# A causal mask added by TensorE instead of selected by GpSimd, for the first two tiles of an mLSTM with two MLP stages

## The chip, the core and the metric

The program runs on one core of a Trainium2 chip. The core's engines have queues of their own and work them in order: TensorE (PE in the profile; its weight loads are PEld), VectorE (DVE), ScalarE (ACT), GpSimd (POOL) and SyncE (SP), which here only starts transfers. They wait for one another by semaphores. The metric is the time of one execution on the device, in microseconds (us).

## The reference

The kernel computes three stages one after the other. First an mLSTM layer with 2 batches, 8 heads, 768 steps and head size 40, then a mixture of 4 experts (320 to 1024 to 320, ReLU, weighted by normalized domain probabilities), then a gated MLP ((x w_a) * (x w_b)) w_out with inner size 1536. The mLSTM is a recurrence over the steps t; what matters here is its gating and its order:

```python
m_new  = max(f[t] + m, i[t])                 # running maximum
f_stab = exp(f[t] + m - m_new);  i_stab = exp(i[t] - m_new)
C = f_stab * C + i_stab * outer(v[t], k[t])
n = f_stab * n + i_stab * k[t]
y[t] = sigmoid(o[t]) * (C q[t]) / max(|n . q[t]|, 1)
```

Step t only sees steps up to t. In a form that works on 128 steps at once this is a causal mask.

## The kernel before

The 1536 rows (2 batches of 768) are 12 tiles of 128 steps; tiles 0 and 1 are the first 128 steps of the two batches. For each tile, and for each half of four heads (`hh`), the kernel makes a 128x512 block of scores k q (`scores`, tile `pt_c`) and a 128x512 block of exponents (`weights_of`, tile `pt_a`): TensorE multiplies `LT`, which holds the gate terms of the key steps, by `Rr`, which holds those of the query steps. ScalarE writes the exponential into `w_t`, GpSimd's `affine_select` sets the entries with a key later than the query to zero, VectorE multiplies by the scores (`s1b`), and TensorE multiplies by the values (`s2a`, tile `pt_y`). VectorE then divides (`s2b`), and three transposes (`s3a`) and a split into a high and a low part (`split_hi`, `split_lo`) give the operand `xh`, `xl` of the expert stage. That stage, and the gated MLP behind it, are long rows of products on TensorE (lines 207 to 263).

The gates come from a chain on VectorE: `gate1` is a scan for the running maximum `mr` along the steps, `gate2` a scan of the logarithmic decay, `gate_hi` and `gate3` split them for TensorE, and `build_R` fills `Rr`, in four calls for the first two tiles (two tiles by two halves). For the first tiles the scan starts from a column that GpSimd writes, line 402: `nc.gpsimd.memset(mr[:, 0:1], NEG)`, within `gate1`.

Order: the kernel runs under a manual schedule, so each engine's queue holds its instructions in the order in which the code writes them. The opening, from line 583 on, is written out by hand, and the rest is a list of events with due times among the expert stage's products. Ahead of the opening's scores stand ten warm-up products (`warm_up(WARM)`, line 590), products of zeros in bf16 whose result nobody reads; `wz`, their operand, lies in the last columns of the tile `sums` (named `acc` in the profile), which is used as a landing place for raw weights and later for the sums of the experts. Single warm-ups stand between later groups. The tile pools in PSUM are `ps_t` (four banks), `ps_a` and `ps_b` (two each).

Of the kernel before, what the change touches and what calls it, by code (L numbers as in the profile page):

```python
# [7 lines left out]
F32 = mybir.dt.float32  # L8
F32R = mybir.dt.float32r
BF16 = mybir.dt.bfloat16  # L10
# [4 lines left out]
ALU = mybir.AluOpType  # L15
# [3 lines left out]
P = 128  # L19
# [18 lines left out]
WARM = 10  # L38
# [3 lines left out]
NEG = -1.0e30  # L42
# [5 lines left out]
def mlstm_moe_kernel(ctx, tc, gates, qk, qc, kvo, dp, w1b, w2b, ident_d, bdmask_d, rsel_d, exp_d, out):  # L48
    nc = tc.nc
# [17 lines left out]
    sums = xp.tile([P, NT * DM], F32, name="acc")  # L67
# [199 lines left out]
    begun = {}  # L267
# [59 lines left out]
    ps_a = ctx.enter_context(tc.tile_pool(name="ps_a", bufs=2, space=PS))  # L327
    ps_b = ctx.enter_context(tc.tile_pool(name="ps_b", bufs=2, space=PS))
    with ExitStack() as c1:
# [4 lines left out]
        ps_t = c1.enter_context(tc.tile_pool(name="ps_t", bufs=4, space=PS))  # L334

        g_sb = {}
        td = {}
# [5 lines left out]
        LT = [ac.tile([G, P], F32R, name=f"LT{i}") for i in range(2)]  # L343
        Rr = [ac.tile([G, H, P], F32R, name=f"Rr{b}") for b in range(B)]
        dec = ac.tile([120, NCH, 3, B], F32, name="dec")

        def load_qk(n, hh, eng=None):

            t = td.setdefault(n, {})
            if 2 <= n < NP:  # L350
                t["qk", hh] = td[n - 2]["qk", hh]
            else:
                tag, bufs = ("qs", 2) if (n, hh) == (1, 1) else ("qk", QB)
                t["qk", hh] = qp.tile([KS, 2, 512], F32, tag=tag, name="qk_t", bufs=bufs)
            v = t["qk", hh].rearrange("p a b -> p (a b)")
            if n < 2:
                (nc.gpsimd if n else nc.vector).memset(v, 0.0)
            r = D if n < NP else KS
            (eng or nc.sync).dma_start(v[0:r], qk[n, hh, 0:r])
# [103 lines left out]
        def build_R(n, eng, h0=0, h1=H):  # L463
            j, b = n // 2, n % 2
            zx = g_sb[j]["zx"]
            eng.tensor_tensor(
                Rr[b][0:64, h0:h1], zx.bitcast(F32).unsqueeze(1).to_broadcast([64, h1 - h0, P]),
                rsel[0:64, b * H + h0:b * H + h1].unsqueeze(2).to_broadcast([64, h1 - h0, P]), op=ALU.mult)

        def weights_of(n, hh, pool=ps_t, tag="t"):  # L470

            j, b = n // 2, n % 2
            td[n]["w", hh] = w = qp.tile([P, 512], F32, tag="w", name="w_t", bufs=4)
            pa = pool.tile([P, 512], F32, tag=tag, name="pt_a")
            nc.tensor.matmul(pa, LT[j % 2], Rr[b][:, 4 * hh:4 * hh + 4, :].rearrange("p h t -> p (h t)"), start=True, stop=True)  # L475
            nc.scalar.activation(w, pa, AF.Exp)
            nc.gpsimd.affine_select(w, w, pattern=[[0, 4], [1, P]], compare_op=ALU.is_ge, fill=0.0, base=0, channel_multiplier=-1)

        def scores(n, hh, pool=ps_t, tag="t"):
            t = td[n]  # L480
            qs = t["qk" if n < NP else "qs", hh]
            t["pc", hh] = pc = pool.tile([P, 512], F32, tag=tag, name="pt_c")
            for h in range(4):
                hs = slice(h * P, (h + 1) * P)
                nc.tensor.matmul(pc[:, hs], qs[:, 1, hs], qs[:, 0, hs], start=True, stop=True, skip_group_check=True)  # L485

        def s1a(n, hh):
            weights_of(n, hh)
            scores(n, hh)
# [5 lines left out]
        def s2a(n, hh):  # L495

            j, b = n // 2, n % 2
            t = td[n]
            kv = t["kvo"]
            if hh == 0:  # L500
                t["py"] = ps_t.tile([P, 512], F32, tag="t", name="pt_y")
            for h in range(4 * hh, 4 * hh + 4):
                nc.tensor.matmul(  # L503
                    t["py"][:, h * DE:h * DE + 2 * DE], t["w", hh][:, (h % 4) * P:(h % 4 + 1) * P],
                    kv[:, NK + h * DE:NK + (h + 2) * DE], start=True, stop=True, skip_group_check=True)
            if hh == 1 and j > 0:
                pi = ps_t.tile([P, 512], F32, tag="t", name="pt_i")
                for g in range(3):
                    nc.tensor.matmul(pi[:, g * 123:(g + 1) * 123], t["qc"][:, g * P:(g + 1) * P], cbd[b][:, g, :], start=True, stop=True, skip_group_check=True)  # L509
                t["pi"] = pi  # L510

        def s2b(n):
            j, b = n // 2, n % 2
            t = td[n]
            r = og[j][:, b].rearrange("p (h d) -> p h d", d=D)
            y = a2.tile([P, H, DE], F32, tag="y", name="y_t", bufs=1)
            pyv = t["py"][:, 0:H * DE].rearrange("p (h e) -> p h e", e=DE)
            if j > 0:
                nc.vector.tensor_tensor(
                    y, t["pi"][:, 0:H * DE].rearrange("p (h e) -> p h e", e=DE),  # L520
                    g_sb[j]["ET"][:, b * H:(b + 1) * H].unsqueeze(2).to_broadcast([P, H, DE]), op=ALU.mult)
                nc.vector.tensor_tensor(y, pyv, y, op=ALU.add)
            else:
                y = pyv
            dn = a2.tile([P, H, 1], F32, tag="dn", name="dn_t")
            nc.vector.tensor_scalar(dn, y[:, :, D:DE], -1.0, 1.0, op0=ALU.mult, op1=ALU.max)
            nc.vector.tensor_tensor(dn, y[:, :, D:DE], dn, op=ALU.max)
            nc.vector.reciprocal(dn, dn)
            x = a2.tile([P, DM + 64], F32, tag="x", name="x_t")
            xv = x[:, :DM].rearrange("p (h d) -> p h d", d=D)  # L530
            nc.vector.tensor_tensor(xv, y[:, :, 0:D], dn.to_broadcast([P, H, D]), op=ALU.mult)
            t["last"] = nc.vector.tensor_tensor(xv, xv, r, op=ALU.mult).ins
            t["x"] = x
# [48 lines left out]

        ctx.enter_context(tc.manual_schedule())
        wz = sums[:, 3520:3776].bitcast(BF16)
        nc.gpsimd.memset(wz, 0.0)

        def warm_up(n):

            for _ in range(n):
                nc.tensor.matmul(pw, wz[:, 0:P], wz, start=True, stop=True)  # L590
# [25 lines left out]
        load_qk(0, 1)  # L616
        load_qk(1, 0)
        load_qk(1, 1)
        for t in LT:
            nc.vector.memset(t[0:64].bitcast(F32), 1.0)  # L620
        nc.sync.dma_start(td[0]["kvo"][:, NK:NK + NV], kvo[0, :, NK:NK + NV])
# [10 lines left out]
        nc.sync.dma_start(bdmask.rearrange("p g e -> p (g e)"), bdmask_d)  # L632
        nc.sync.dma_start(dpt.rearrange("p n e -> p (n e)"), dp)
        pw = ps_a.tile([P, 512], F32, tag="a", name="pt_w")
        warm_up(WARM)
        scores(0, 0)
        scores(0, 1)
        gate1(0, V)
        for b in range(B):
# [5 lines left out]
        for n in range(2):  # L645
            build_R(n, V, 0, 4)
            build_R(n, V, 4, 8)
        weights_of(0, 0, ps_b, "b")
        weights_of(0, 1, ps_b, "b")
        scores(1, 0)  # L650
        weights_of(1, 0, ps_a, "a")
        weights_of(1, 1, ps_b, "b")
        scores(1, 1)
        go(w1[:2])
        load_qk(2, 0)
# [11 lines left out]
        s2a(0, 0)  # L667
        s2a(0, 1)
        s2b(0)
        warm_up(1)  # L670
        s2a(1, 0)
        s2a(1, 1)
        warm_up(1)
# [74 lines left out]
        for k in range(NI * NCH):  # L748
            until(k)
            j, i = k // NI, k % NI  # L750
# [168 lines left out]
```

## Time and profile before

| | |
|---|---|
| median of 3 runs | 635.52 us (635.47 to 637.03) |
| the profiled execution's own time | 635.51 us |
| its span, first to last instruction | 633.8 us |
| PE busy, share of the span | 621.0 us, 98% |
| DVE | 419.4 us, 66% |
| ACT | 266.7 us, 42% |
| POOL | 186.0 us, 29% |
| chain that ended last, PE's share | 90% |

The busy shares are means over stages with different limits. From about 62 us on TensorE has work all the time; before that the mLSTM's first tiles pass through all engines in turn, and the engines wait for one another. The change is in the first 18 us. There the views that count are the timelines of the single engines: a row there gives start, length, engine, line, operation and what it reads and writes, and in brackets the idle time ahead of it and what ended that.

### The profile page before, as it was taken

Reading aid. Unit: us, or ns where it says so; the run is one execution under the profiler, and the core shown is the slowest. Engines: PE = TensorE matmul, PEld = TensorE weight load, DVE = VectorE, ACT = ScalarE, POOL = GpSimd, SP = SyncE. Lnnn points to the kernel's source line nnn. Section 1 sums busy time; section 2 is a strip of 40 time slices with the busy share of each in tenths; the row PEclk is TensorE's granted clock in tenths of the full one; section 3 lists DMA queues with packets and bytes.
Section 4 is the critical chain, followed back from the end, with each engine's and each line's share of the span. In section 5 each row is a group of like instructions: output and inputs, shape, how many; then the busy total and the mean of one; then the engine's idle time right before and its main releaser. Section 6 shows DMA issues by size and latency. Waiting matters only on the chain.

```text
span 633.8 us, 10305 instructions
## 1 busy us (share of the span) xinstructions
PE 621.0 (98%) x3799; PEld 553.1 (87%) x3799; DVE 419.4 (66%) x860; ACT 266.7 (42%) x592; POOL 186.0 (29%) x223
## 2 busy tenths in 40 slices
PE   9898999999999999999999999999999999999997
PEld 6788999999999888888888888888888888888886
DVE  8889959596753244332788887888656776854344
ACT  6665464646333233332433344544543433422121
POOL 4686342424111011233233333333222222220000
PEclk9998999999999999999999999999999999999999
DMA  7882443435203122323221222221111111000003
GB/s 218 240 231 74 116 118 95 120 99 125 55 12 78 35 69 58 79 59 109 57 71 54 71 57 68 70 64 44 45 54 35 55 36 35 19 1 1 1 3 123
DMA packets 27967, 46.77 MB, mean 74 GB/s; under 512 B 3285, under 2 KB 17869, under 8 KB 27917
## 3 DMA queue, kind: packets, MB, share of 16 engines
q1 hardware_dynamic: 27437, 45.33, 26.2%
q0 software_dynamic: 480, 0.79, 0.6%
q8 instruction: 30, 0.49, 0.3%
q14 instruction: 20, 0.16, 0.1%
HBM read 43.35 MB, written 1.97 MB: 72 GB/s over the span
## 4 chain that ended last, share of the span: by engine, by line
PE 90%; DVE 6%; ACT 2%; issue 1%; POOL 1%; ACTq 0%; DVEq 0%; POOLq 0%
PE psa L214 20%; PE psa L207 14%; PE psy L261 13%; PE psy L263 11%; PE psy L262 11%; PE psb L214 8%; PE pt_y L503 3%; PE pt_c L485 2%; PE psb L207 2%; PE psb L219 1%; PE psa L219 1%; PE pt_i L509 1%; PE pt_a L475 1%; PE pt_w L590 1%; PE pt_u L553 1%
## 5 line engine op out<-in xcount | busy, mean ns | idle before, releaser
L261 PE MATMUL psy<-wh,hh 128*128 128x320 f32 x528 | 169.1, 320 | 0.6 <-DVE acc L321 0.6
L263 PE MATMUL psy<-wh,hl 128*128 128x320 f32 x528 | 163.2, 309 | 0.0
L262 PE MATMUL psy<-wl,hh 128*128 128x320 f32 x528 | 163.1, 309 | 0.0
L261 PEld LDWEIGHTS psy<-wh,hh 128*128 128x128 f32 x528 | 99.6, 189 | 15.5 <-issue 12.1
L262 PEld LDWEIGHTS psy<-wl,hh 128*128 128x128 f32 x528 | 99.7, 189 | 2.6
L263 PEld LDWEIGHTS psy<-wh,hl 128*128 128x128 f32 x528 | 99.4, 188 | 0.0
L307 DVE SCALAR_TENSOR_TENSOR hl<-psa,hh 128x512 fp32r<-128x512 f32 x60 | 40.2, 689 | 74.4 <-ACT hh L306 73.9
L124 POOL TENSOR_TENSOR wl<-tp,lf 128x272 fp32r<-128x272 f32 x48 | 38.8, 808 | 122.2 <-DVE tp L123 122.2
L214 PE MATMUL psa<-xh,wh 128*128 128x512 f32 x246 | 70.1, 393 | 0.0
L207 PE MATMUL psa<-xh,wh 128*128 128x256 f32 (+1 forms) x258 | 65.8, 309 | 0.4 <-ACT xh L132 0.4
L306 ACT ACTIVATE hh<-psa 128x512 fp32r<-128x512 f32 x60 | 34.5, 597 | 72.4 <-PE psa L214 41.3
L207 PE MATMUL psa<-xh,wl 128*128 128x256 f32 (+1 forms) x258 | 63.9, 302 | 0.0
L237 ACT ACTIVATE hh<-psa 128x256 fp32r<-128x256 f32 x72 | 27.6, 383 | 75.0 <-PE psa L207 73.5
L312 DVE TENSOR_TENSOR g<-psa,bs 128x512 f32<-128x512 f32 x36 | 24.8, 688 | 49.3 <-ACT bs L310 35.0
L121 POOL TENSOR_TENSOR lf<-lf,sq 128x272 f32<-128x272 f32 x48 | 37.2, 776 | 67.8 <-ACT wh L120 34.0
L92 POOL TENSOR_TENSOR wl<-raw,wh 128x352 fp32r<-128x352 f32 x28 | 26.6, 956 | 96.4 <-ACT wh L90 83.9
L214 PE MATMUL psa<-xh,wl 128*128 128x512 f32 x164 | 51.2, 393 | 0.0
L214 PE MATMUL psa<-xl,wh 128*128 128x512 f32 x164 | 50.8, 391 | 0.0
L238 DVE SCALAR_TENSOR_TENSOR hl<-psa,hh 128x256 fp32r<-128x256 f32 x72 | 30.3, 420 | 30.7 <-ACT hh L237 30.4
L214 PEld LDWEIGHTS psa<-xh,wh 128*128 128x128 f32 x246 | 44.0, 188 | 6.0
L310 ACT COPY bs<-psb 128x512 f32<-128x512 f32 x36 | 21.1, 587 | 62.7 <-PE psa L220 35.0
L207 PEld LDWEIGHTS psa<-xh,wh 128*128 128x128 f32 x258 | 45.2, 191 | 2.1 <-ACT xh L132 0.7
(139 smaller groups left out, 1168.0 us busy)
## 6 DMA issues: line engine op xcount, KB each, us to landing
raw<-in_w2b SPq DMA_DIRECT2D x48, 272.0 KB, 2.8
qk_t<-in_qk SPq DMA_DIRECT2D x16, 480.0 KB, 6.9
raw<-in_w1b SPq DMA_DIRECT2D x40, 176.0 KB, 2.3
acc<-in_w1b SPq DMA_DIRECT2D x24, 176.0 KB, 3.5
kvo_t<-in_kvo SPq DMA_DIRECT2D x10, 364.5 KB, 4.8
og_t<-in_kvo SPq DMA_DIRECT2D x6, 320.0 KB, 5.7
out<-acc SPq DMA_DIRECT2D x12, 160.0 KB, 1.8
qc_t<-in_qc SPq DMA_DIRECT2D x10, 180.0 KB, 3.6
```

Source lines behind the costliest of these rows:

```text
L92: lo_eng.tensor_tensor(wl[:, cs], raw, wh[:, cs].bitcast(F32), op=ALU.subtract)
L121: nc.gpsimd.tensor_tensor(lf, lf, sq, op=ALU.mult)
L124: nc.gpsimd.tensor_tensor(wl[:, cs], tf, lf, op=ALU.add)
L207: nc.tensor.matmul(ps, l, r, start=(i == 0), stop=(i == len(prs) - 1))
L214: nc.tensor.matmul(ps, k(w, t), x[c][:, u, :], start=start and i == 0, stop=not start and i == len(prs) - 1)
L237: nc.scalar.activation(self.hh, ps, AF.Relu)
L238: nc.vector.scalar_tensor_tensor(self.hl, ps, 0.0, self.hh.bitcast(F32), op0=ALU.max, op1=ALU.subtract)
L261: nc.tensor.matmul(ps, lh, wh[:, off:off + DM], start=(fi == 0), stop=False)
L262: nc.tensor.matmul(ps, lh, wl[:, off:off + DM], start=False, stop=False)
L263: nc.tensor.matmul(ps, ll, wh[:, off:off + DM], start=False, stop=(fi == nf - 1))
L306: nc.scalar.activation(it.hh, ps, AF.Relu)
L307: nc.vector.scalar_tensor_tensor(it.hl, ps, 0.0, it.hh.bitcast(F32), op0=ALU.max, op1=ALU.subtract)
```

## The change

For tiles 0 and 1 the mask is no longer selected on `w_t` by GpSimd. Instead a block `mneg` (zero where the key is not later than the query, -1e30 elsewhere, bf16) is multiplied by an identity `idb` (bf16) into the bank `pt_a` first (`mask`), and the exponents product adds to it (`start=False`). GpSimd makes `mneg` and `idb` with two memsets and three selects, which the code writes behind the loads of q and k. Three masks take the place of three of the ten warm-ups, the fourth stands ahead of the last exponents product. The scores of tile 1's first half are issued in three parts (one head, one head, two heads) between the exponents products, and a warm-up between the value products of the two tiles is gone.

```diff
-            pa = pool.tile([P, 512], F32, tag=tag, name="pt_a")
-            nc.tensor.matmul(pa, LT[j % 2], Rr[b][...], start=True, stop=True)
+            begun = td[n].pop(("pa", hh), None)
+            pa = begun or pool.tile([P, 512], F32, tag=tag, name="pt_a")
+            nc.tensor.matmul(pa, LT[j % 2], Rr[b][...], start=not begun, stop=True)
             nc.scalar.activation(w, pa, AF.Exp)
+            if begun:
+                return
             nc.gpsimd.affine_select(w, w, pattern=[[0, 4], [1, P]], compare_op=ALU.is_ge, fill=0.0, base=0, channel_multiplier=-1)
+        def mask(n, hh, pool, tag):
+            td[n]["pa", hh] = pa = pool.tile([P, 512], F32, tag=tag, name="pt_a")
+            nc.tensor.matmul(pa, idb, mneg, start=True, stop=False)
...
+        mneg = sums[:, 3168:3424].bitcast(BF16)
+        idb = sums[:, 3776:3840].bitcast(BF16)
...
         load_qk(1, 1)
+        nc.gpsimd.memset(mneg, 0.0)
+        nc.gpsimd.affine_select(mneg, mneg, pattern=[[0, 4], [1, P]], compare_op=ALU.is_ge, fill=NEG, base=0, channel_multiplier=-1)
+        nc.gpsimd.memset(idb, 1.0)
+        nc.gpsimd.affine_select(idb, idb, pattern=[[1, P]], compare_op=ALU.is_ge, fill=0.0, base=0, channel_multiplier=-1)
+        nc.gpsimd.affine_select(idb, idb, pattern=[[-1, P]], compare_op=ALU.is_ge, fill=0.0, base=0, channel_multiplier=1)
...
-        warm_up(WARM)
+        warm_up(WARM - 3)
+        mask(0, 0, ps_b, "b")
+        mask(0, 1, ps_b, "b")
+        mask(1, 0, ps_a, "a")
         scores(0, 0)
         scores(0, 1)
         gate1(0, V)
...
-        weights_of(0, 0, ps_b, "b")
-        weights_of(0, 1, ps_b, "b")
-        scores(1, 0)
-        weights_of(1, 0, ps_a, "a")
-        weights_of(1, 1, ps_b, "b")
+        weights_of(0, 0)
+        scores(1, 0, h1=1)
+        weights_of(0, 1)
+        scores(1, 0, h0=1, h1=2)
+        weights_of(1, 0)
+        scores(1, 0, h0=2)
+        mask(1, 1, ps_b, "b")
+        weights_of(1, 1)
         scores(1, 1)
...
         s2b(0)
-        warm_up(1)
         s2a(1, 0)
```

GpSimd's queue before, from its first memset in the kernel on (`acc` at line 585 is the warm-ups' operand, `ISA` stands for pool configuration):

```order
L585 MEMSET acc 128x512
L607 MEMSET rmask 112x128
L608 MEMSET rmask 112x1
L357 MEMSET qk_t 120x1024 x2
L402 MEMSET mr 112x1
L477 ISA
L477 AFFINE_SELECT w_t<-w_t 128x512 x4
```

And the same place in the changed kernel, where lines 631 to 635 write `mneg` and `idb`, both named `acc`:

```order
L620 MEMSET rmask 112x1
L357 MEMSET qk_t 120x1024 x2
L631 MEMSET acc 128x512
L632 ISA
L632 AFFINE_SELECT acc<-acc 128x512
L633 MEMSET acc 128x128
L634 AFFINE_SELECT acc<-acc 128x128
L635 AFFINE_SELECT acc<-acc 128x128
L402 MEMSET mr 112x1
L92 TENSOR_TENSOR wl_147<-acc,wh_146 128x352 x5
```

The configuration and five new instructions stand ahead of the memset of `mr`, which stood ahead of them; the four selects on `w_t` are gone.

TensorE's queue before, from the last warm-up ahead of the scores to the value products of the two tiles (with buffer numbers; `Rr0` is of tile 0, `Rr1` of tile 1):

```order
L590 MATMUL pt_w_159<-acc_81 128x512
L485 MATMUL pt_c_170<-qk_t_123 128x128 x4
L485 MATMUL pt_c_175<-qk_t_126 128x128 x4
L475 MATMUL pt_a_209<-Rr0_108,LT0_106 128x512
L475 MATMUL pt_a_214<-Rr0_108,LT0_106 128x512
L485 MATMUL pt_c_218<-qk_t_129 128x128 x4
L475 MATMUL pt_a_224<-Rr1_109,LT0_106 128x512
L475 MATMUL pt_a_229<-Rr1_109,LT0_106 128x512
L485 MATMUL pt_c_233<-qk_t_132 128x128 x4
```

And in the changed kernel (line 485 there is the mask product, 476 the exponents, 495 the scores):

```order
L485 MATMUL pt_a_178<-acc_81 128x512
L495 MATMUL pt_c_180<-qk_t_123 128x128 x4
L495 MATMUL pt_c_185<-qk_t_126 128x128 x4
L476 MATMUL pt_a_174<-Rr0_108,LT0_106 128x512
L495 MATMUL pt_c_221<-qk_t_129 128x128
L476 MATMUL pt_a_176<-Rr0_108,LT0_106 128x512
L495 MATMUL pt_c_221<-qk_t_129 128x128
L476 MATMUL pt_a_178<-Rr1_109,LT0_106 128x512
L495 MATMUL pt_c_221<-qk_t_129 128x128 x2
L485 LDWEIGHTS acc_81
L485 MATMUL pt_a_232<-acc_81 128x512
L476 MATMUL pt_a_232<-Rr1_109,LT0_106 128x512
```

The exponents products are spread between the scores of tile 1's first half, and a mask product stands ahead of the last of them.

## Rows read from the trace of the kernel before

**Rows 1.** Chain of waits, first 20 us: start, length (us), what.

```profile
1.39 4.45 PE pt_w L590 x10
...
15.23 0.18 DVE dn_t L526
```

**Rows 2.** Timeline of VectorE, first 22 us: start, length, engine, line, operation.

```profile
3.47 0.48 DVE L406 TENSOR_TENSOR_SCAN mr<-gt,mr 112x128 f32<-112x128 f32 x1
...
7.39 2.49 DVE L466 TENSOR_TENSOR Rr<-zx,rsel 64x512 fp32r<-64x512 f32 x4
10.41 2.61 DVE L493 TENSOR_TENSOR w_t<-pt_c,w_t 128x512 f32<-128x512 f32 x4 [0.54 <-POOL w_t L477]
...
15.23 0.17 DVE L526 TENSOR_SCALAR dn_t<-pt_y 128x8 f32<-128x8 f32 x1 [0.23 <-PE pt_y L503]
```

**Rows 3.** Timeline of GpSimd, first 22 us.

```profile
0.81 0.53 POOL L585 MEMSET acc<- 128x512 bf16 x1 [0.29 <-POOLq L907]
1.26 0.21 POOL L607 MEMSET rmask<- 112x128 f32 x1
1.53 0.10 POOL L608 MEMSET rmask<- 112x1 f32 x1
...
3.34 0.10 POOL L402 MEMSET mr<- 112x1 f32 x1
9.39 2.89 POOL L477 TENSOR_SCALAR_AFFINE_SELECT w_t<-w_t 128x512 f32<-128x512 f32 x4 [5.96 <-ACT w_t L476]
```

**Rows 4.** Line 477, first 12 us: operation, ns min/median/max, first and last start.

```profile
L477 POOL TENSOR_SCALAR_AFFINE_SELECT w_t<-w_t x4: 634/638/983, 9.4 to 11.6; 128x512 f32<-128x512 f32 x4
L477 POOLq MODIFY_POOL_CONFIG  x2: 13/13/13, 3.4 to 3.4; - x2
```

**Rows 5.** Timeline of TensorE, first 22 us.

```profile
1.39 4.45 PE L590 MATMUL pt_w<-acc 128*128 128x512 bf16 x10 [1.39 <-POOL acc L585]
5.70 2.63 PE L485 MATMUL pt_c<-qk_t 120*128 120x128 f32 x16
8.21 1.02 PE L475 MATMUL pt_a<-Rr,LT 112*128 112x512 f32 x2
...
9.88 0.71 PE L475 MATMUL pt_a<-Rr,LT 112*128 112x512 f32 x2
10.43 1.05 PE L485 MATMUL pt_c<-qk_t 120*128 120x128 f32 x8
11.32 1.91 PE L503 MATMUL pt_y<-kvo_t,w_t 128*128 128x82 f32 x16
13.07 0.38 PE L590 MATMUL pt_w<-acc 128*128 128x512 bf16 x1
...
15.57 1.03 PE L590 MATMUL pt_w<-acc 128*128 128x512 bf16 x4
```

**Rows 6.** Timeline of ScalarE, first 45 us.

```profile
8.72 1.14 ACT L476 ACTIVATE w_t<-pt_a 128x512 f32<-128x512 f32 x2 [2.18 <-PE pt_a L475]
...
27.47 0.49 ACT L90 CAST wh<-acc 128x352 fp32r<-128x352 f32 x1 [1.66 <-DMA acc<-in_w1b]
```

**Rows 7.** Stretches: busy us (instructions) of each engine, granted clock, transfers.

```profile
core 0: us, PE busy (x) PEld busy (x) DVE busy (x) ACT busy (x) POOL busy (x), PEclk, DMA share, GB/s
6.00:7.00 1.00, 1.00 (x6) 1.00 (x6) 0.90 (x4) 0.52 (x2) 0.00 (x0) 1.00 0.95 221
7.00:8.00 1.00, 1.00 (x11) 1.00 (x11) 0.95 (x3) 0.00 (x0) 0.00 (x0) 1.00 1.04 233
...
58.00:62.00 4.00, 4.00 (x19) 4.00 (x20) 3.97 (x3) 1.62 (x4) 2.85 (x2) 0.57 0.00 0
62.00:66.00 4.00, 4.00 (x32) 3.89 (x31) 3.72 (x10) 1.78 (x6) 0.90 (x1) 1.00 0.86 207
```

**Rows 8.** Timeline of TensorE, first 60 us: its two long waits.

```profile
24.45 0.30 PE L454 MATMUL pt_e<-ident,ex 96*128 96x96 f32 x1 [1.99 <-ACT ex L444]
...
57.20 0.79 PE L457 MATMUL pt_e<-eb,expd 16*120 16x2 f32 x6 [2.54 <-POOL eb L448]
```

**Rows 9.** Timeline of SyncE, first 22 us.

```profile
15.14 0.90 SPq L86 DMA_DIRECT2D acc<-in_w1b  x2
```

More of the change, by code (lines that the diff above doesn't have):

```diff
@@ L473, in weights_of, with scores @@
             td[n]["w", hh] = w = qp.tile([P, 512], F32, tag="w", name="w_t", bufs=4)
-            pa = pool.tile([P, 512], F32, tag=tag, name="pt_a")
-            nc.tensor.matmul(pa, LT[j % 2], Rr[b][:, 4 * hh:4 * hh + 4, :].rearrange("p h t -> p (h t)"), start=True, stop=True)
+            begun = td[n].pop(("pa", hh), None)
+            pa = begun or pool.tile([P, 512], F32, tag=tag, name="pt_a")
+            nc.tensor.matmul(pa, LT[j % 2], Rr[b][:, 4 * hh:4 * hh + 4, :].rearrange("p h t -> p (h t)"), start=not begun, stop=True)
             nc.scalar.activation(w, pa, AF.Exp)
+            if begun:
+                return
             nc.gpsimd.affine_select(w, w, pattern=[[0, 4], [1, P]], compare_op=ALU.is_ge, fill=0.0, base=0, channel_multiplier=-1)
-        def scores(n, hh, pool=ps_t, tag="t"):
+        def mask(n, hh, pool, tag):
+            td[n]["pa", hh] = pa = pool.tile([P, 512], F32, tag=tag, name="pt_a")
+            nc.tensor.matmul(pa, idb, mneg, start=True, stop=False)
+        def scores(n, hh, pool=ps_t, tag="t", h0=0, h1=4):
             t = td[n]
             qs = t["qk" if n < NP else "qs", hh]
-            t["pc", hh] = pc = pool.tile([P, 512], F32, tag=tag, name="pt_c")
-            for h in range(4):
+            if h0 == 0:
+                t["pc", hh] = pool.tile([P, 512], F32, tag=tag, name="pt_c")
+            pc = t["pc", hh]
+            for h in range(h0, h1):
                 hs = slice(h * P, (h + 1) * P)
```

## The prediction

> **What bounds the kernel now.** I read the chain of waits first, over the first 20 us, since every instruction the change touches stands there. It is named almost wholly by TensorE: warm-up products from 1.39, the scores, the exponents, the value products, and from 15.23 VectorE's division [rows 1]. TensorE's own line hides a second chain that is as tight, so I read VectorE's timeline next. It has one gap of half a microsecond: the gate scan of the first two tiles starts at 3.47, the four builds of R end at 9.88 (7.39 + 2.49), the four products of scores and weights run from 10.41 to 13.02, and only the 0.54 us ahead of the latter are a wait, for GpSimd's mask [rows 2]. TensorE gets its first exponents product only at 8.21, after the first build of R (7.39 + 0.62 = 8.01); had it been quicker before, it would have waited there. So in this stretch the gate scan on VectorE sets the rest, and the question is what starts that scan.
>
> GpSimd's timeline answers it: it writes the first column of the running maximum (L402) at 3.34 to 3.44, right behind its two memsets of q and k, and the scan, which reads that column, starts 0.03 us after it [rows 2, 3]. The scan has no slack against GpSimd. Between that small memset and the first mask at 9.39 GpSimd shows 5.96 us of idle time. The line's own view shows what lies in it: two pool configuration instructions at 3.4, 13 ns each, which the program places ahead of the first select [rows 3, 4].
>
> **What the change removes.** Four selects of 0.64 to 0.98 us leave the way between exponential and product [rows 4]. VectorE's first product of scores and weights no longer waits until 10.41; it can follow the last build of R at 9.88. But TensorE does not wait for these products: it runs without a gap from the exponents product at 9.88 over the last scores (10.43) and the value products from 11.32 on, whose first operand would now be there at 10.6 and before was there at 11.1 [rows 2, 5]. So only what TensorE has to do itself counts. The exponents product of the last half tile still waits for the last R; ahead of it stand now, behind the R before (9.25, ready for TensorE at 9.45, as 8.21 followed 8.01), an exponents product (0.21), two heads of scores (0.44, half of the 0.89 from 10.43 to 11.32) and a mask (0.21): 10.31, where it could start at 10.08. The scores behind it start at 10.52, 0.09 later than before; the warm-up at 13.07 between the value products is gone (0.21; the same figure for a mask comes from the group of four warm-ups, (1.03 - 0.38) / 3). The gain at the second division is thus 0.1 to 0.2 us; I take 0.2. The three masks ahead of the scores replace three warm-ups of the same shape and cost nothing, as long as their operands are there.
>
> **What it adds, and where.** Five GpSimd instructions now stand ahead of the small memset L402. A memset of 128x512 bf16 took 0.53; a select of 512 elements 0.64 when nothing disturbed it; a memset of 128 elements 0.21; two selects of 128 elements lie between 0.10 (the shortest GpSimd row) and 0.64, and I take 0.25, near the quarter of the long one [rows 3, 4]. Each waits for the one before: 1.53 against 1.26 + 0.21 gives 0.06, three times. Sum 0.53 + 0.64 + 0.21 + 0.50 + 0.18 = 2.06, bounds 1.8 to 3.2. Queued behind them on GpSimd is the memset that the gate scan waits for, and behind the scan the whole of VectorE's queue. So the gate chain is late by 2.1 us from this alone.
>
> With the first select the pair of configuration instructions also moves ahead of that memset. What they set going has no row of its own. The bounds: nothing (their rows are 13 ns), or all the time up to the first select, whose start was at 9.39 and which took 0.35 longer than its fellows; 9.39 + 0.35 - 3.4 = 6.3 us [rows 3, 4]. I take 6.0, by the 5.96 us idle row: it is the only one in which this pair is followed by a select, under the same DMA load. Before, this time lay beside VectorE's gate work (3.47 to 8.01) and ScalarE's first exponential (from 8.72 on), so it cost nothing; that cover is gone now, because the memset for the scan stands behind it [rows 2, 6].
>
> The Trainium skill, "GPSIMD Engine Reference", section "Instruction dispatch", says that the first call to a freshly loaded kernel pays some 6 us (5.95 measured) for loading code, without an instruction in the profile. By that figure the sum below would be 643.15; this case's trace cannot confirm it, it only leaves room for it.
>
> The scan is late by 2.1 + 6.0 = 8.1; of the first memset's 0.53 some may lie beside the loading, so I take 8.0. It starts at 11.5, the first R is there at 16.0.
>
> TensorE meanwhile: seven warm-ups at 0.43 end at 4.4, then it has nothing until the identity is ready, at about 11.3. It will be at 1.2 GHz again or still: in the trace before, the warm-ups came 0.43 apart from 1.39 on, and the score products went from six starts in the microsecond 6 to 7 to eleven in the next, after 5.6 us of unbroken work (the granted clock column reads 1.00 from the start, so I go by the spacing of the rows) [rows 5, 7]. At that rate three masks (1.3) and 16 score instructions at 0.21 (3.4) take it from 11.3 to 16.0. The first R comes at 16.0 too, so the slow rate is just hidden; I add 0.2 for the products right behind it.
>
> **The sum.** 8.0 - 0.2 + 0.2 = +8.0 at the second division. Little downstream absorbs it: VectorE, ScalarE and GpSimd work their queues in order, and what shifts with them ends TensorE's two long waits (2.0 for ScalarE's exponential at 24.45, 2.5 for GpSimd at 57.20) [rows 8]. Only work that waits for a transfer gains; there is one such wait, 1.66 us on ScalarE ahead of 27.47, and it is not on the chain [rows 6]. I take 0.3 back for it. SyncE's queue holds one transfer (the second piece of block 1) until the last mask product has read its operand, near 18.7 instead of its issue before 16.04 [rows 9]; what is behind it (q and k of the next tiles) is late by about 3 us, less than its readers. From about 62 us on TensorE is the bound [rows 7], and it keeps the shift to the end. The profiled execution took 635.51 with a span of 633.8 (the median of the runs is 635.52): 635.51 + 8.0 - 0.3 = 643.2.
>
> **Rivals.**
> *The loading is short or is no loading at all.* Then only the 2.1 us of GpSimd work is late: 2.1 - 0.2 - 0.3 = +1.6, 637.1, which is within 0.3% (1.9 us; about what a measurement of this kernel can tell from no change). For it: the configuration rows are 13 ns, and the idle row is put down to ScalarE's exponential, which begins at 8.72 and, with a pair in 1.14, ends only shortly before the select. Against it: nothing in the trace runs on GpSimd in these 6 us, so it shows no short load either. It decides below about 0.3 us of loading. Chance 0.13. In between, a load of 0.3 to 4.5 us gives 637.4 to 641.6: 0.10.
>
> *TensorE's clock becomes the bound.* After 7 us without work, and with gaps while it waits for each R, it may stay at 1.2 GHz through the last scores and the value products: 0.89 + 3.5 us of work at twice the time is up to +4.4; half of that gives 645.4. For it: 16 scores took 2.63 where later eight took 1.05 [rows 5]. Against it: from 11.3 to 16 it has unbroken work as it had before 7.0. Chance 0.11.
>
> *Faster.* The set-up is hidden after all, the 0.2 is kept, and the low clock at 58 to 62 (0.57 granted, 19 instructions where the next 4 us have 32) does not come back, because the wait ahead of it falls otherwise: at the half rate that is (1 - 0.57) x 4 = 1.7 us at most [rows 7]. Time 635.5 - 0.2 - 1.7 = 633.6, just over 0.3%. It needs the scan not to wait for GpSimd; 0.03 us of slack speak against that. Chance 0.04.
>
> **Numbers.** Forecast: 643.2, chance 0.62, its own range 641.2 to 645.2 (loading 4.5 to 6.3, the low clock at 58 us gone or doubled). The range for 8 in 10 reaches down into the middle case, to 638.0, and up into the clock case, to 645.5; left out are the short load and the faster case (0.17) and a little above. Faster 0.04; within 0.3% 0.11; slower 0.85.
>
> **What would show it.** In the changed profile: a row of GpSimd's first select at or after 9.3, not at 4; the small memset behind it at about 11; VectorE's scan at about 11.5 with an idle time of 8 us ended by GpSimd; TensorE idle from 4.4 to about 11; the four products of scores and weights directly behind the builds of R, waiting for nothing on GpSimd; the second division at 22 to 23. If the first select starts near 4 and the scan at 5.6, the loading term is wrong. If the scan is at 3.5, the order of GpSimd's queue doesn't matter and the prediction fails at its root. If the scan is late as said and the end is not, something downstream had slack that I did not see.

## The result and the profile after

The changed kernel takes 639.22 us (median of 12 executions, 637.63 to 644.33), the kernel before 637.0 us (12 executions, 635.45 to 638.91) in the same comparison: ratio 1.0052, interval 1.0028 to 1.0076. It is slower by about 2.2 us at the median, not by 7.7; the mean rises by 3.3 us (636.70 to 639.95), since more executions lie on high steps. The times of both lie on steps: before 635.5, 637.05 and 638.8; after 637.65, 639.2, 641.0, 642.4 and 644.3. The lowest step rose by 2.2 us (637.63 against 635.45). The profiled execution of after took 639.18 with a span of 637.4, so it lies on the second step.

GpSimd's timeline, which answers to [rows 3]; start, length, engine, line, operation:

```profile
3.34 0.53 POOL L631 MEMSET acc<- 128x512 bf16 x1
3.94 0.64 POOL L632 TENSOR_SCALAR_AFFINE_SELECT acc<-acc 128x512 bf16<-128x512 bf16 x1
4.52 0.21 POOL L633 MEMSET acc<- 128x128 bf16 x1
4.79 0.29 POOL L634 TENSOR_SCALAR_AFFINE_SELECT acc<-acc 128x128 bf16<-128x128 bf16 x1
5.16 0.29 POOL L635 TENSOR_SCALAR_AFFINE_SELECT acc<-acc 128x128 bf16<-128x128 bf16 x1
5.40 0.10 POOL L402 MEMSET mr<- 112x1 f32 x1
```

The memset that the gate scan waits for is at 5.40, not at 3.34 [rows 3]. The first select starts at 3.94 and not at 9.4 or later. The view of its line shows the pair of configuration instructions right ahead of it (operation, ns min/median/max, first and last start):

```profile
L632 POOLq MODIFY_POOL_CONFIG  x2: 16/16/16, 3.8 to 3.8; - x2
...
L632 POOL TENSOR_SCALAR_AFFINE_SELECT acc<-acc x1: 637/637/637, 3.9 to 3.9; 128x512 bf16<-128x512 bf16 x1
```

VectorE's timeline, against [rows 2]:

```profile
5.53 0.48 DVE L406 TENSOR_TENSOR_SCAN mr<-gt,mr 112x128 f32<-112x128 f32 x1 [2.18 <-POOL mr L402]
...
9.45 2.49 DVE L466 TENSOR_TENSOR Rr<-zx,rsel 64x512 fp32r<-64x512 f32 x4
11.86 2.68 DVE L503 TENSOR_TENSOR w_t<-pt_c,w_t 128x512 f32<-128x512 f32 x4
...
15.53 0.17 DVE L536 TENSOR_SCALAR dn_t<-pt_y 128x8 f32<-128x8 f32 x1 [0.99 <-PE pt_y L513]
...
17.31 0.17 DVE L536 TENSOR_SCALAR dn_t<-pt_y 128x8 f32<-128x8 f32 x1
```

The scan is late by 2.06 (5.53 against 3.47), the first build of R by 2.06 (9.45 against 7.39), the second division by 2.08 (17.31 against 15.23). The wait for GpSimd's mask ahead of the products (0.54 before) is gone, as the change means it to be, and nothing comes of it at the second division.

TensorE's timeline, against [rows 5, 8]:

```profile
1.39 3.17 PE L602 MATMUL pt_w<-acc 128*128 128x512 bf16 x7 [1.39 <-POOL acc L597]
5.51 1.46 PE L485 MATMUL pt_a<-acc 128*128 128x512 bf16 x3 [0.95 <-POOL mr L402]
6.76 3.62 PE L495 MATMUL pt_c<-qk_t 120*128 120x128 f32 x16
10.28 0.71 PE L476 MATMUL pt_a<-Rr,LT 112*128 112x512 f32 x1
...
12.69 1.05 PE L495 MATMUL pt_c<-qk_t 120*128 120x128 f32 x8
...
26.64 0.30 PE L454 MATMUL pt_e<-ident,ex 96*128 96x96 f32 x1 [2.00 <-ACT ex L444]
...
27.58 1.86 PE L495 MATMUL pt_c<-qk_t 120*128 120x128 f32 x8
...
60.95 0.79 PE L457 MATMUL pt_e<-eb,expd 16*120 16x2 f32 x6 [2.55 <-POOL eb L448]
```

The masks wait 0.95 us for the identity. (The profile names L402, GpSimd's last instruction before they start; what they read is written by L635, which ends at 5.45.) Sixteen scores take 3.62 instead of 2.63, but the first exponents product follows its R as closely as before: 10.28 after a build that starts at 9.45, against 8.21 after 7.39. So the slow scores are hidden. Eight scores take 1.86 at 27.58, where eight took 1.05 before [rows 5]. Stretches (as [rows 7]) show why:

```profile
core 0: us, PE busy (x) PEld busy (x) DVE busy (x) ACT busy (x) POOL busy (x), PEclk, DMA share, GB/s
...
28.00:32.00 4.00, 4.00 (x24) 4.00 (x24) 2.41 (x4) 1.66 (x5) 4.00 (x5) 0.59 0.47 132
58.00:62.00 4.00, 1.45 (x12) 1.22 (x11) 3.96 (x5) 1.70 (x5) 3.92 (x5) 1.00 0.10 36
62.00:66.00 4.00, 4.00 (x21) 3.97 (x20) 3.94 (x4) 1.45 (x4) 2.61 (x2) 0.58 0.00 0
```

The granted clock is 0.59 from 28 to 32 us, behind the 2.00 us wait that ends at 26.64. VectorE's instructions are 2.2 us behind those of before up to 27 us and 3.7 us behind from 45 us to the end: that fall costs 1.5 us, the height of one step of the times. The low stretch at 62 to 66 is the one that stood at 58 to 62 before [rows 7].

### The profile page after: what moved, and what is told of

It reads as the page before. It is cut to its first block, busy times and chain, and to the rows that moved or that the text cites. A ratio compares the mean times of both kernels' runs of the same rounds, so it can differ in the third digit from the quotient of the medians.

```text
span 637.4 us, 10300 instructions
## 1 busy us (share of the span) xinstructions
PE 623.8 (98%) x3798; PEld 555.9 (87%) x3799; DVE 419.0 (66%) x860; ACT 266.9 (42%) x592; POOL 185.3 (29%) x224
## 4 chain that ended last, share of the span: by engine, by line
PE 90%; DVE 5%; ACT 2%; POOL 1%; DMA 1%; issue 1%; ACTq 0%; POOLq 0%; DVEq 0%
PE psa L214 20%; PE psa L207 14%; PE psy L261 12%; PE psy L263 11%; PE psy L262 11%; PE psb L214 8%; PE pt_y L513 3%; PE pt_c L495 2%; PE psb L207 2%; PE psb L219 2%; PE psa L219 1%; DMA gt<-in_gates 1%; PE pt_i L519 1%; PE pt_a L476 1%; PE pt_u L563 1%
```

## The experiments

Ratios are to the kernel before, executed beside each; e12 is a single execution. Two theories stood for the 2.2 us. By the queue theory the scan is late since five instructions stand ahead of its memset. By the TensorE theory the masks wait for their operands, and the scores then run at half rate.

**e1, the memset first.** On the changed kernel, line 402's memset goes ahead of the five:

```diff
...
         load_qk(1, 1)
+        mr0 = a2.tile([G, P + 1], F32, tag="mr", name="mr")
+        nc.gpsimd.memset(mr0[:, 0:1], NEG)
         nc.gpsimd.memset(mneg, 0.0)
```

> The changed kernel with only GpSimd's small memset for the scan (first column of mr) moved ahead of the five set-up instructions; the masks on TensorE still wait for the set-up. Queue theory (the late scan is the whole loss): scan back at 3.47, second division at 15.2 to 15.4, time at the level of the kernel before (635.5 where TensorE's clock falls once, 637.0 where it falls twice). TensorE theory (its scores, late behind the masks and at the half rate until 10.8, hold it as much as the scan does): first exponents product still at 10.2 to 10.3, second division at 16.7 to 17.0, time 637.0 to 637.4 with one fall of the clock.

Lowest time 636.04, median 639.18, ratio 1.0025 (1.0004 to 1.0046). The second division is at 15.72, 0.3 behind the range of the queue theory and 1.0 ahead of that of the TensorE theory. VectorE's timeline and GpSimd's beside it show what is left:

```profile
3.47 0.48 DVE L404 TENSOR_TENSOR_SCAN mr<-gt,mr 112x128 f32<-112x128 f32 x1
3.99 0.76 DVE L407 TENSOR_TENSOR lf<-gt,mr 112x128 f32<-112x128 f32 x1
4.78 0.29 DVE L408 TENSOR_TENSOR lf<-lf,mr 112x128 f32<-112x128 f32 x1
...
7.86 1.28 DVE L464 TENSOR_TENSOR Rr<-zx,rsel 64x512 fp32r<-64x512 f32 x2
```

```profile
3.97 0.63 POOL L632 TENSOR_SCALAR_AFFINE_SELECT acc<-acc 128x512 bf16<-128x512 bf16 x1
...
4.83 0.40 POOL L634 TENSOR_SCALAR_AFFINE_SELECT acc<-acc 128x128 bf16<-128x128 bf16 x1
```

The scan is back at 3.47. The instruction behind it takes 0.76 us instead of 0.29, beside GpSimd's select, and R comes 0.47 late for that reason. At the lowest step 1.6 of the 2.2 us are thus the memset's place (637.63 to 636.04); the median stays, since ten of the twelve executions lie on higher steps.

**e2, the set-up earlier.** The memset of `mr` and the five go ahead of the memsets of q and k, and the loads of tile 1 go later.

```diff
...
         nc.gpsimd.memset(rmask[:, 0:1], 0.0)
+        mr0 = a2.tile([G, P + 1], F32, tag="mr", name="mr")
+        nc.gpsimd.memset(mr0[:, 0:1], NEG)
+        nc.gpsimd.memset(mneg, 0.0)
...
-        load_qk(1, 0)
-        load_qk(1, 1)
...
         nc.sync.dma_start(td[1]["kvo"][:, NK:NK + NV], kvo[1, :, NK:NK + NV])
+        load_qk(1, 0)
+        load_qk(1, 1)
```

> The changed kernel with mr's memset and the whole set-up moved ahead of GpSimd's two memsets of tile 1's q and k, whose loads go behind those of the first values. Both theories: masks right behind the warm-ups at 4.4, scan at 3.4 to 3.5, first exponents product at about 8.2, second division at 15.0 to 15.2, 635.3 to 635.5 with one fall of the clock, so 2.1 to 2.3 under the changed kernel. If it stays above 15.6, the exponents, scores and masks in their new order cost TensorE something of their own, or the later loads of tile 1 do (then a wait ahead of its first scores shows it).

Lowest 635.95, median 637.62, ratio 1.0004 (0.9986 to 1.0023). The second division is at 15.91, above the 15.6 of the expectation, for two reasons. The collision only moves: VectorE's line 415 takes 0.59 instead of 0.23, beside GpSimd's memsets of q and k, which now start at 3.65.

```profile
4.97 0.59 DVE L415 TENSOR_SCALAR lf<-lf 112x128 f32<-112x128 f32 x1
```

```profile
3.65 1.84 POOL L357 MEMSET qk_t<- 120x1024 f32 x2
```

R comes 0.36 late by it (7.75). And the later loads of tile 1 cost what the expectation named as their sign, a wait ahead of its first scores:

```profile
9.39 0.46 PE L493 MATMUL pt_c<-qk_t 120*128 120x128 f32 x2 [0.33 <-DMA qk_t<-in_qk]
```

**e3, the delay alone.** The kernel before with four memsets of 128x512 ahead of line 402, and nothing else of the change:

```diff
...
         load_qk(1, 1)
+        for _ in range(4):
+            nc.gpsimd.memset(sums[:, 3168:3424].bitcast(BF16), 0.0)
```

> The kernel before, with four memsets of 128x512 bf16 on GpSimd (some 2.2 us) ahead of mr's memset and nothing else. Queue theory: scan at 5.7, second division 2.2 later than before (17.4), 637.7 with one fall of the clock: the loss of the change without any of its masks. TensorE theory: TensorE is free at 8.3 here, so only the scan counts, also 17.4. If the selects that the change removes were worth 0.2 behind a late scan, this kernel is 0.2 to 0.4 slower than the changed one, whose scan is 0.15 earlier. If VectorE's lateness were absorbed somewhere downstream, the time would stay under 637.

Median 642.97 (638.18 to 644.93), ratio 1.0066 (1.0041 to 1.0091). The delay alone costs more than the change, and more than the 637.7 that was expected. The scan is at 5.68; then TensorE waits 2.56 us for the first R, and its clock falls:

```profile
10.42 1.01 PE L475 MATMUL pt_a<-Rr,LT 112*128 112x512 f32 x2 [2.56 <-DVE Rr L466]
11.26 1.82 PE L485 MATMUL pt_c<-qk_t 120*128 120x128 f32 x8
```

```profile
11.00:15.00 4.00, 4.00 (x18) 3.77 (x19) 2.48 (x5) 2.48 (x5) 2.35 (x4) 0.57 1.02 332
```

The lowest time is 2.7 us above the kernel before, 0.5 more than the delay of R (9.59 against 7.39); the median is 4.8 higher still, since the clock falls (e9 below separates the two). In the profile of after no such wait stands ahead of R: the slow scores fill it.

**e4, ten warm-ups.** e1 with ten warm-ups instead of seven, to fill the wait ahead of the masks:

```diff
-        warm_up(WARM - 3)
+        warm_up(WARM)
```

> As the first of these (mr's memset ahead of the set-up), with ten warm-ups instead of seven ahead of the masks, so that TensorE works without a gap from 1.4. Queue theory: like that one, 15.2 to 15.4. TensorE theory, by the rate: the rate rises near 7.0 as in the kernel before, scores end at 8.8 to 9.0, second division at 15.5 to 15.8, about 1.2 us earlier than with seven warm-ups, 635.8 to 636.1 with one fall of the clock. TensorE theory, by the late masks alone: no earlier than with seven warm-ups (16.7 to 17.0), since three more products stand in the queue.

Lowest 636.01, median 637.61, ratio 1.0009 (0.9992 to 1.0026). The second division is at 15.71, within what the TensorE theory by the rate had named, but that theory asked for 1.2 us less than with seven warm-ups, and e1 has 15.72. The gap ahead of the masks costs nothing up to there, so the TensorE theory falls in this form. The median is 1.6 us under e1's; the two intervals overlap, so whether the gap brings on falls of the clock later stays open.

**e5, no selects.** What is the removal of the selects worth at most? This kernel leaves out the causal mask of tiles 0 and 1 altogether.

```diff
             nc.scalar.activation(w, pa, AF.Exp)
+            if n < 2:
+                return
             nc.gpsimd.affine_select(w, w, pattern=[[0, 4], [1, P]], compare_op=ALU.is_ge, fill=0.0, base=0, channel_multiplier=-1)
```

> The kernel before with the causal mask of tiles 0 and 1 left out altogether (no select, no mask product): what the removal alone is worth. Theory of the recorded prediction (TensorE's own work from the last R to the second division sets the time, the selects lie beside it): VectorE's four products start at 9.9 instead of 10.4, second division at 15.0 to 15.25, 635.3 to 635.5 with one fall of the clock. Rival (the select was on the way): second division at 14.2 to 14.7, 634.5 to 635.0.

Lowest 635.49, median 638.08, ratio 1.0009 (0.9992 to 1.0025). VectorE's products follow R without a wait, 0.62 us earlier than before, and the second division stays where it was (15.22 against 15.23):

```profile
9.79 2.50 DVE L495 TENSOR_TENSOR w_t<-pt_c,w_t 128x512 f32<-128x512 f32 x4
...
15.22 0.17 DVE L528 TENSOR_SCALAR dn_t<-pt_y 128x8 f32<-128x8 f32 x1 [0.24 <-PE pt_y L505]
```

TensorE sets that division, and the selects were hidden beside it. Their removal had nothing to win there.

**e6, the change without its cost.** The mask in 128 columns, read four times; its set-up ahead of the memsets of q and k; one of these on ScalarE; the first head of tile 1's scores ahead of the first exponents.

```diff
...
+            if (n, hh) == (1, 1):
+                nc.scalar.copy(v.rearrange("p (a b) -> p a b", b=256), sums[0:KS, 3520:3776].unsqueeze(1).to_broadcast([KS, 4, 256]))
...
+            nc.tensor.matmul(pa.rearrange("p (h t) -> p h t", h=4), idb, mneg.unsqueeze(1).to_broadcast([P, 4, P]), start=True, stop=False)
...
-        weights_of(0, 0)
         scores(1, 0, h1=1)
+        weights_of(0, 0)
```

> The changed kernel with the scan's memset first, the mask set-up in 128 columns instead of 512 (the product reads it four times), done ahead of GpSimd's memset of tile 1's first q and k, the second of these memsets on ScalarE, and the first head of tile 1's scores ahead of the first exponents product. So GpSimd has nothing left beside VectorE's gate chain. If the late scan (2.1) and GpSimd's slowing of VectorE's two-operand instructions (0.47 in the kernel with mr's memset first) were the whole loss: scan at 3.4 to 3.6, first build of R at 7.4 to 7.5, second division at 14.9 to 15.2, 635.2 to 635.5 with one fall of the clock, no or hardly any gain over the kernel before. If the removal is worth more than that, under 635.0. If something else in the change costs time, above 635.9.

Lowest 635.55, median 636.42, ratio 0.9997 (0.9976 to 1.0018). Scan at 3.45, R at 7.36, second division at 15.23: the loss is gone, and no gain stands in its place.

```profile
3.45 0.49 DVE L406 TENSOR_TENSOR_SCAN mr<-gt,mr 112x128 f32<-112x128 f32 x1
...
15.23 0.17 DVE L536 TENSOR_SCALAR dn_t<-pt_y 128x8 f32<-128x8 f32 x1
```

**e7 and e8, the two long waits filled.** To see whether the steps are falls of the clock behind TensorE's waits for ScalarE and GpSimd [rows 8], products of zeros of 256 columns go into both, 16 into the first and 20 into the second; e7 on the kernel before, e8 on the changed one.

```diff
+            for _ in range(16 if j == 1 else 0):
+                nc.tensor.matmul(pt[:, 256:512], wz[:, 0:P], wz[:, 0:256], start=True, stop=True, skip_group_check=True)
             nc.tensor.transpose(pt[:, 0:96], ex[0:96, :], ident[0:96, 0:96])
+            for _ in range(20 if j == 2 else 0):
+                nc.tensor.matmul(pt[:, 256:512], wz[:, 0:P], wz[:, 0:256], start=True, stop=True, skip_group_check=True)
```

> The kernel before with zero products of 256 columns put into TensorE's two long waits: 16 ahead of the wait that ends at 24.45 and 20 in the one that ends at 57.20, some 0.11 us each at the full rate (1.7 and 2.1 of 2.0 and 2.5 us). Theory (the steps of 1.5 to 1.8 us between runs are stretches at the half rate that these two waits bring on): the runs lie closer together, most of them at the lowest level or under it, median 635.5 or less (down to 633.8 where the fall at 58 us is gone too). Rival (the rate falls for another reason): same levels and spread as before, median near 637, plus what the products cost where they overrun.

> The changed kernel with the same zero products in the same two waits. If the loss is the 2.1 us at the start alone and the rest of the difference of the medians came from the clock: 2.1 to 2.3 above the kernel before with these products, run for run at the same level, with the spread gone. If the change brings on more low stretches at another place: the spread stays here and not there.

e7: median 635.51 (635.44 to 635.94), ratio 0.9973 (0.9960 to 0.9987): every execution on the lowest step. e8: median 637.70 (637.56 to 639.28), ratio 1.0017 (1.0001 to 1.0033); seven on 637.6, five on 639.2. Between the two medians lie 2.19 us, and VectorE's instructions in e8 are 2.06 us behind those of e7 at the second division and 2.17 behind at their last (rows under e9). That is the price of the late scan by itself. Between the means lie 2.74 us (638.28 and 635.54), since e8 has a second step that e7 has not (e10 and e12 below).

e7's profile also tells what the low clock at 58 to 62 was worth, since there is none:

```profile
57.22 0.79 PE L461 MATMUL pt_e<-eb,expd 16*120 16x2 f32 x6 [0.37 <-POOL eb L448]
...
61.81 0.50 PE L207 MATMUL psa<-xl,wh 128*128 128x256 f32 x2 [1.30 <-DVE xl L135]
```

```profile
58.00:62.00 4.00, 2.70 (x20) 2.50 (x20) 3.97 (x3) 1.62 (x4) 2.88 (x2) 1.00 0.00 0
```

At the full clock TensorE gets to line 207 earlier and waits 1.30 us there for VectorE. The time is the same with that fall and without it (635.51 in the profiled execution of before [rows 7], 635.50 in e7's): it cost nothing.

**e9, the delay with all waits filled.** e3 with the products of e7 and ten warm-ups in the wait for R:

```diff
...
             build_R(n, V, 4, 8)
+        warm_up(10)
         weights_of(0, 0, ps_b, "b")
```

> The kernel before with the late scan (four memsets on GpSimd, scan 2.2 late) and zero products in three waits: the two long ones of the earlier runs, and ten warm-ups in the 2.56 us wait for the first R that the late scan opens. If the delay of the scan passes on one to one and the rest of that kernel's loss (638.2 at its lowest, 642.97 median) was the clock: all runs at 637.6 to 637.8, 2.1 to 2.3 above the kernel before with its two waits filled (635.5). If they stay at 638.2, half a microsecond more is lost behind a late scan when the selects are still there, and the change's removal of them is worth that in its own, late, frame.

Median 638.15 (638.04 to 638.46), ratio 1.0008 (0.9992 to 1.0025). That is the 638.2 of the expectation's second case, not the 637.6 to 637.8 of its first. The upper steps of e3 are gone, and the granted clock from 11 to 15 us is 1.00 instead of 0.57:

```profile
11.00:15.00 4.00, 4.00 (x33) 3.89 (x34) 3.44 (x6) 3.43 (x7) 3.31 (x5) 1.00 1.03 321
```

The scan is 2.20 us late (5.67), and VectorE's last instructions are 2.19 late; they stand here for e7, e8 and e9:

```profile
628.89 1.81 DVE L787 TENSOR_TENSOR acc<-psy,acc 128x320 f32<-128x320 f32 x4 [0.48 <-PE psy L263]
```

```profile
631.06 1.81 DVE L809 TENSOR_TENSOR acc<-psy,acc 128x320 f32<-128x320 f32 x4 [0.49 <-PE psy L263]
```

```profile
631.08 1.81 DVE L790 TENSOR_TENSOR acc<-psy,acc 128x320 f32<-128x320 f32 x4 [0.48 <-PE psy L263]
```

So the late scan alone (e9) puts the end of the work where the change puts it (e8), within 0.02 us. The selects were worth nothing behind a late scan either: from the first build of R to the second division it is 7.85 us in e9, with them, and 7.86 in e8, without. The time of e9 is 2.64 above e7. The other 0.4 us arises behind VectorE's last instruction, where only the last output transfers and the end of the program remain: the span ends 3.5 us behind it in e9 (636.4), 3.1 in e7 (633.8) and in e8 (636.0). In e3 it is 3.7 us against 3.1 in before. Why that takes longer there isn't shown.

**e10 and e12, the second step of e8.** e10 is e8 with ten warm-ups (the edit of e4), against the gap ahead of the masks; e12 is the same kernel again, for a trace of the second step.

> The changed kernel with zero products in the two long waits and ten warm-ups instead of seven, so that TensorE has no gap ahead of the masks either. If the five of twelve runs at 639.2 with only the two waits filled came from that gap: all runs at 637.6 to 637.9. If they came from elsewhere: still some at 639.2.

> The kernel of e10 once more, to find its second level, 639.2 us at a mean granted clock of 0.996, where e7 has none. If the long waits at lines 456 and 461 are still what lowers TensorE's rate although zero products stand ahead of them, a run at 639.2 shows a stretch at about 0.58 granted within 6 us behind one of them (26 to 34 us, or 58 to 66 us). The rival is that an opening wait does it (1.2 us ahead of the first exponents product, or the two of 1.0 us ahead of the transposes): then the low stretch begins between 9 and 24 us and VectorE's instructions behind it are 3.6 us behind those of e7 instead of 2.1. A run at 637.6 shows neither and leaves it open.

e10: median 639.12 (637.60 to 639.37), ratio 1.0019 (1.0005 to 1.0033), five on 637.6 and seven on 639.2; so that gap isn't the cause. e10's profile fell on the lower step. In it, TensorE waits 1.18 us for the first R, and no clock falls behind that:

```profile
6.90 2.18 PE L499 MATMUL pt_c<-qk_t 120*128 120x128 f32 x16
10.26 0.47 PE L480 MATMUL pt_a<-Rr,LT 112*128 112x512 f32 x1 [1.18 <-DVE Rr L470]
...
12.67 1.05 PE L499 MATMUL pt_c<-qk_t 120*128 120x128 f32 x8
```

e12 took 639.03, the upper step:

```profile
6.15 1.95 PE L499 MATMUL pt_c<-qk_t 120*128 120x128 f32 x16
10.26 0.47 PE L480 MATMUL pt_a<-Rr,LT 112*128 112x512 f32 x1 [2.16 <-DVE Rr L470]
...
13.75 1.38 PE L499 MATMUL pt_c<-qk_t 120*128 120x128 f32 x8
```

```profile
10.00:11.00 1.00, 0.74 (x4) 0.72 (x5) 1.00 (x3) 0.23 (x1) 0.00 (x0) 1.00 1.07 349
11.00:12.00 1.00, 1.00 (x4) 0.84 (x4) 1.00 (x3) 0.94 (x2) 0.00 (x0) 0.50 1.04 311
...
14.00:15.00 1.00, 1.00 (x9) 1.00 (x9) 0.00 (x0) 0.98 (x3) 0.00 (x0) 0.79 1.00 338
```

The rate rose earlier in this execution (the ten warm-ups take 3.69 us instead of 4.45, and the scores start at 6.15 instead of 6.90), so the scores were done earlier and the wait for R was 2.16 us; behind it the granted clock was 0.50, the lower of its two levels (1.2 GHz), from 11 to past 14 us. The first division comes 1.4 us later than in e10, and VectorE's last instruction is still 1.3 us later. So the late scan can have a second price: the wait that it leaves on TensorE, behind which the clock fell in this execution. The rival was right here, the two filled waits are not the cause. That the other executions on the upper step of e10 are of this kind is likely and not shown; in e8, with seven warm-ups, the place of the fall was not seen.

**e11, e6 with the waits filled** (the edits of e6 and e7 together).

> The kernel with the small set-up out of the way of VectorE's gate chain (635.6 at its lowest), with zero products in the two long waits. Shows without the clock's steps what the change is worth at best: if nothing, 635.5 to 635.7, level with the kernel before with the same products (635.5); if the mask by a product is worth more once its set-up is hidden, under 635.3.

Median 635.53 (635.40 to 635.79), ratio 0.9974 (0.9960 to 0.9988): level with e7, by 0.02 us at the median. With its cost taken away and the clock steady, the change is worth nothing. A tenth may be hidden in that: in e11 TensorE waits for the load of tile 1 ahead of the first exponents product, which starts at 8.33 instead of 8.21.

```profile
8.11 0.46 PE L499 MATMUL pt_c<-qk_t 120*128 120x128 f32 x2 [0.17 <-DMA qk_t<-in_qk]
```

e7 and e11 beat both kernels, the one before by 1.6 us at the median, and the change has no part in that.

## Why the prediction was right, and where it was wrong

**The place and the mechanism were right.** The order of GpSimd's queue sets VectorE's scan. The five instructions were put at 2.06, and the scan came 2.06 late; that it fits to the hundredth is luck, since the two short selects took 0.29 and not 0.25 each and the gaps between the instructions came to as much less. That the order is the cause is shown by e1 and e6, which take it away, and by e3 and e9, which add it alone.

**The step that failed is "what the pair of configuration instructions sets going", 6.0 us.** It took some 0.1: the pair is at 3.8, the first select at 3.94. The idle row of 5.96 us [rows 3] was what the profile called it, a wait for ScalarE's exponential, and the rival "the loading is short" had read it so. The prediction gave that rival a chance of 0.13 and took nearly the largest figure that the rows allowed (6.0 of 6.3). The mistake is one of reading: an idle time with a named releaser bounds a hidden cost from above and is no estimate of it. That leaves 2.06 of the 8.1 us of lateness. The forecast difference was 7.7 us to the lowest step of before and is 2.2.

**That the time lies within the stated range is luck.** The range, 638.0 to 645.5, holds the measured 639.22. Its lower part was there for a load of 0.3 to 4.5 us, and there was none; the rival without a load, at 637.1, was left out of it. From the lowest step (635.51), from which the forecast counts, the changed kernel comes to 637.63, half a microsecond from that rival and below the range. The 1.6 us from there to the median are a step of TensorE's clock, which the sum did not have: the median of twelve executions of the kernel before is not at 635.51 either, but at 637.0. The direction, slower, was right for the first of the two reasons given.

The Trainium skill, "GPSIMD Engine Reference", section "Instruction dispatch", was cited there for some 6 us. It speaks of a freshly loaded kernel's first call; the trace has some 0.1 us between the configuration and the first select of this program, so that price does not show at this instruction. Whether a select is such a call no run here shows, nor does any show a first call of another kind.

**The gain of 0.2 at the second division was 0.** From the first build of R to the second division it is 7.84 before, 7.86 after and 7.86 in e1. e5 shows that the selects lay wholly beside TensorE's work, as argued. The 0.2 was the time of the warm-up between the value products, and that was won: 1.78 us lie between the two divisions instead of 1.96. But the mask and the split scores cost as much ahead of the first: the last scores start 3.24 us behind the first build of R (12.69) instead of 3.04 (10.43). The prediction had 0.09 for this.

**The half rate (0.2) and the absorption downstream (0.3).** Both measured 0: the slow scores were hidden by the wait for R, as forecast, with nothing behind them; and the 2.1 at the second division is 2.2 at the end (e8). e10 shows the hiding best: its scores are done early, TensorE waits 1.18 us for R, and the first exponents product starts at 10.26 all the same.

**The rival on the clock** was right in kind and small. It had TensorE at half rate through the last scores and the value products for half of 4.4 us; in the profile of after this stretch ran at 1.00, and e12, whose kernel has three more warm-ups, shows the fall with 1.4 us. The steps of 1.4 to 1.9 us between executions are of this size; e7 shows that those of the kernel before come from the later waits. Both kernels have such steps, so the medians still differ by the 2.2 of the lateness; the changed kernel has more of them, and the means differ by 3.3.

**The "faster" rival** priced the low clock at 58 to 62 at 1.7 us. It was worth 0 (e7): VectorE would have been waited for instead.

**What the prediction named as its refutation came**: "If the first select starts near 4 and the scan at 5.6, the loading term is wrong." They were at 3.94 and 5.53.

## What to carry to other kernels

Before an operation goes to another engine, look at what is queued behind the place where its set-up goes: here one memset of 0.1 us behind five new instructions held up three engines, while the operation that was taken away lay beside work that took as long. Read an idle row with a named releaser as that wait first; a load that may hide in it needs a row of its own before it stands in a sum. Where times of one kernel lie on steps, compare step with step, look for TensorE's waits of some 2 us, and try cheap products in them.

## What the runs showed that was not expected

GpSimd slows VectorE where the two overlap in certain instructions: 0.76 instead of 0.29 us for an instruction with two operands in SBUF beside a select that reads SBUF (e1), 0.59 instead of 0.23 for a one-operand instruction beside a memset (e2). Not every overlap does it: the three two-operand instructions ahead of that one in e2 took 0.29 each beside the same memsets, and in e1 the next two-operand instruction (4.78) took its 0.29 while the select that started behind it (4.83) took 0.40 instead of 0.29. The Trainium skill, "SBUF — State Buffer", section "Who interferes with whom", has the two engines share a pair of ports that one holds for a whole instruction. In e1 VectorE's instruction ends at 4.75, 0.15 behind the select's end at 4.60; a full block would have put it at 4.60 + 0.29 = 4.89. The rows agree with the rule in kind and show a little less than a full block.

TensorE's clock fell behind waits of 2.0 to 2.6 us in the profiles of before, after, e3 and e12, and not behind one of 1.18 (e10); nor behind every long one, since none followed the 1.99 us of [rows 8]. Thirty-six small products of zeros in two waits took the spread of twelve executions from 635.46 to 640.56 (35 executions of the kernel before, in the same comparison) down to 635.44 to 635.94.
